# Windowed attention and a soft mixture of experts: re-ordered steps, sums from a column of ones, masks written by TensorE, and a second layer by column halves

## The chip, the cores and the metric

One core of a Trainium2 chip. The metric is device time of one execution in microseconds, from start to end of the program; the times of the kernel before are three runs, and one execution was recorded by the hardware profiler. All data begin and end in device memory. The core's engines are TensorE (PE; PEld is its weight load), VectorE (DVE), ScalarE (ACT), GpSimd (POOL) and SyncE (SP), which here issues all transfers. Every engine works through its own list of instructions in order.

## The reference

```
q, k, v: (4, 8, 768, 64);  n_sink = 4, window = 128
scores = q @ k.T / 8;  keep key p for query s if p < 4 or 0 <= s - p < 128
a = softmax(scores);   att = a @ v                     # (4, 8, 768, 64)
x = att.transpose(0, 2, 1, 3).reshape(3072, 512)
logits = x @ phi                                       # (3072, 32): 8 experts x 4 slots
d = softmax(logits over the 3072 tokens);  slot_input = d.T @ x        # (32, 512)
h = relu(slot_input[e] @ w1[e]);  slot_out[e] = h @ w2[e]              # F = 1024
out = softmax(logits over the 32 slots) @ slot_out                     # (3072, 512) f32
```

Inputs and outputs are f32. The expert weights are 2 x 16 MB of f32, the output is 6 MB.

## The kernel before, in words

**Attention** runs in 12 jobs (batch b of 4, and j of 3 blocks of 256 queries; `window_path`, from L694). A job loads k, q and v in blocks of 128 rows (`load`, 256 KB each), transposes k and q on PE into `kt` and `qt` (`prep`), and makes four score tiles (`softmax`: `quad` is the group of heads, `odd` the half of a block's queries). For each tile PE makes the scores, DVE masks them in PSUM and takes the row maxima (`maxima`), ACT takes four exponentials with their row sums (`exps`: an ACTIVATE and a read of the accumulator each), DVE adds the sinks' share and inverts the sums (`inverse`), POOL multiplies the tile by the inverses (128x528, key `N`) and copies out the sink columns (`sinks`). In jobs with j = 0 there are no earlier keys, and DVE fills those columns with a large negative number by MEMSET. Then PE transposes the weights (`weights_transposed`), POOL cuts them to the window (`select`: 8 AFFINE_SELECT in a job, 7 where j = 0), PE multiplies them by v (`values`), and the result x is turned back (`natural`).

**Router** (`Moe.tokens`, L348), still inside the job: logits, running maxima over tokens, the exponentials with their sum (`zb`), the products d.T @ x added up in `acc` (`sums`), and the running sum `z` (`totals`). `finish` (L439) makes the slots' inputs; `slot_softmax`, `stack` and `turn` make the weights with which the output is combined.

**Order.** Nothing of this is issued as written. Each step is entered in `Plan` with a key, engines on which it may run ("AV" means ACT or DVE), a time, and what it reads and writes; `Plan.order` (L175) plays the steps through, takes at each point the free engine that can start first and the ready step of the lowest key, and so sets each engine's list and the engine of a step that has a choice. The keys are the hand-made numbers of `CFG`. The helper at L129 issues every planned instruction, so that nearly all of the profile has that one line.

**Weights** come as 32 tiles of 1 MB in the order of `Weights` (L639), into SBUF tiles of 1 MB (`slot`, 22 of them, and the two tiles `first` in which k, q, x and x's transpose lie during attention). 18 are issued before attention ends, the rest as its tiles become free.

**Tail** (`tail`, L552), in the written order: layer 1 (64 matmuls of 512 columns, tiles 0 to 15), relu, transposes of h into `ht`, layer 2 (`second`: one step is four matmuls of 512 columns side by side in four column groups; expert groups r = 0, 1, and k = 0 to 7 in each; the last four k by column halves, from tiles 28 to 31, each of which holds all columns of two experts for two k). Its result, 32 slots x 512, is split into a rounded part and a remainder for both halves (L620 on ACT, L621 on DVE), and 24 products of 48 matmuls make the output: one for each 128 tokens, copied from PSUM by ACT and DVE in turn (L635), and stored by 2 transfers of 512 KB and 5 of 1 MB (L636).

## Time and profile before

| | us |
|---|---|
| median of 3 runs (lowest, highest) | 240.36 (239.79, 242.28) |
| profiled execution, its own time | 240.57 |
| its span in the trace | 238.9 |
| PE busy, share of the span | 203.1, 85% |
| DVE, ACT, POOL busy | 157.3, 147.7, 140.4 |
| transfers, mean over the span | 249 GB/s |

The trace covers 238.9 of the 240.57 us; 1.67 us lie outside it. Rows below give starts in us from the start of the span. A group such as `ps<-wt` names what an instruction writes and reads: `ps` is PSUM, `wt` any tile from `slot`, `first` the two tiles of k, q and x. A releaser after `<-` is what ended the idle time before an instruction. Idle time of an engine that is not the bottleneck costs nothing. Matmuls run at two records for each f32 instruction, so that counts of PE in the trace are about twice those of the program.

### The profile page before, as it was taken

The page shows a single profiled execution, that of the slowest core. Times are in us where ns is not written, and L with a number is a line of the kernel's source. Part 1 is how long each engine was busy: PE and PEld are TensorE (multiplying, and loading weights), DVE is VectorE, ACT ScalarE, POOL GpSimd, SP SyncE. Part 2 cuts the span into 40 slices and gives each one's busy share as a digit, 9 for nine tenths or more (in the row PEclk, how much of TensorE's full clock was granted, in tenths as well). Part 3 has the DMA queues.
Part 4 walks back from the last instruction along what each step waited for, and adds up shares of the span by engine and source line. Part 5 has one row for each costly group of instructions (what it writes and reads, how often), then busy time and mean ns, then how long its engine had stood idle before and what let it go on. Part 6 is the DMA issues. An engine that isn't in the chain of part 4 may idle for free.

```text
span 238.9 us, 9509 instructions
## 1 busy us (share of the span) xinstructions
PE 203.1 (85%) x3754; PEld 143.5 (60%) x3754; DVE 157.3 (66%) x444; ACT 147.7 (62%) x584; POOL 140.4 (59%) x281
## 2 busy tenths in 40 slices
PE   7864999998999889999999999989699999987600
PEld 7844676876768575768677676857375325236600
DVE  4198878779898967999987999896327105005800
ACT  2187487977889878788987778996325103005600
POOL 2018799793998887698978698989933320000000
PEclk9997699999999999999999999999899999998965
DMA  5596968789998899598999999793549999922994
GB/s 118 118 178 137 255 189 196 291 192 292 276 209 241 217 345 203 190 227 243 208 348 214 296 265 201 255 408 114 176 144 420 375 420 416 411 110 86 399 394 187
DMA packets 84502, 59.49 MB, mean 249 GB/s; under 512 B 76260, under 2 KB 76260, under 8 KB 82916
## 3 DMA queue, kind: packets, MB, share of 16 engines
q1 hardware_dynamic: 84452, 58.83, 81.8%
q8 instruction: 31, 0.51, 0.9%
q14 instruction: 19, 0.16, 0.2%
HBM read 52.53 MB, written 6.29 MB: 246 GB/s over the span
## 4 chain that ended last, share of the span: by engine, by line
PE 52%; DVE 18%; DMA 8%; ACT 7%; issue 7%; POOL 2%; SPq 0%; DVEq 0%; ACTq 0%; POOLq 0%
PE ps L129 51%; DMA wt<-in_moe_w_dram 8%; DVE wt L129 6%; DVE ps L129 5%; ACT wt L129 4%; POOL wt L129 2%; PE ps L1254 2%; DVE rs L129 1%; DVE wt L635 1%; DVE first L129 1%; DVE sums L129 1%; DVE acc L129 1%; ACT pt L129 1%; ACT qt L129 1%; DVE qt L129 0%
## 5 line engine op out<-in xcount | busy, mean ns | idle before, releaser
L129 PE MATMUL ps<-wt 64*64 64x192 f32 (+6 forms) x1214 | 58.2, 314 | 2.8 <-DVE wt L621 1.5
L129 POOL TENSOR_TENSOR wt<-wt 128x528 f32<-128x528 f32 (+1 forms) x72 | 47.1, 663 | 21.1 <-DVE wt L129 15.1
L129 POOL TENSOR_SCALAR_AFFINE_SELECT wt<-wt 128x512 f32<-128x512 f32 x88 | 53.6, 637 | 5.3 <-ACT wt L129 4.8
L129 ACT ACTIVATE wt<-ps,wt 128x132 f32<-128x132 f32 x144 | 51.3, 375 | 8.7 <-DVE wt L129 7.1
L129 PEld LDWEIGHTS ps<-wt 64*64 64x64 f32 (+3 forms) x1214 | 40.8, 137 | 17.0 <-issue 6.9
L129 PE MATMUL ps<-wt,qt 64*64 64x196 f32 (+2 forms) x780 | 46.7, 333 | 3.3 <-ACT qt L129 2.1
L129 PEld LDWEIGHTS ps<-wt,qt 64*64 64x64 f32 x780 | 30.1, 138 | 14.6 <-ACT wt L129 4.9
L129 DVE TENSOR_REDUCE wt<-ps 128x4 f32<-128x528 f32 x48 | 34.0, 707 | 1.7
L129 ACT COPY wt<-ps 128x512 f32<-128x512 f32 x42 | 24.2, 594 | 16.2 <-PE ps L129 12.7
L129 ACT ACTIVATION_READ_ACCUMULATOR wt<-ps,wt 128x1 f32 x144 | 30.2, 210 | 0.0
L129 PE MATMUL ps<-ident,wt 64*128 64x64 f32 (+1 forms) x370 | 25.7, 241 | 3.5 <-DVE wt L129 3.1
L129 PE MATMUL ps<-ident,first 64*128 64x64 f32 (+1 forms) x560 | 25.5, 230 | 3.0 <-ACT wt L129 1.1
L129 PEld LDWEIGHTS ps<-ident,wt 64*128 64x128 f32 (+1 forms) x370 | 20.3, 146 | 11.4 <-POOL wt L129 6.8
L129 PEld LDWEIGHTS ps<-ident,first 64*128 64x128 f32 (+1 forms) x560 | 21.9, 141 | 6.4 <-ACT wt L129 2.3
L129 DVE COPY first<-ps 128x512 f32<-128x512 f32 x23 | 15.6, 686 | 12.3 <-PE ps L129 11.9
L129 DVE COPY_PREDICATED ps<-later,ps 128x256 f32<-128x256 uint8 x48 | 20.3, 423 | 2.7 <-PE ps L129 1.5
L129 DVE COPY wt<-ps 128x512 f32<-128x512 f32 x30 | 20.2, 683 | 1.9 <-PE ps L129 1.1
L129 ACT COPY first<-ps 128x512 f32<-128x512 f32 x25 | 14.9, 601 | 9.4 <-issue 6.9
L129 ACT ACTIVATE pt<-ps,wt 128x132 f32<-128x132 f32 x48 | 17.3, 386 | 1.5 <-DVE wt L129 1.2
L129 POOL TENSOR_TENSOR pt<-pt,wt 128x528 f32<-128x528 f32 x12 | 13.1, 1090 | 1.6 <-ACT wt L129 0.8
L129 PE MATMUL ps<-wt,si 128*32 128x512 f32 x120 | 13.9, 593 | 0.0
L129 PE MATMUL ps<-first,phi 128*32 128x128 f32 x384 | 13.4, 276 | 0.3
(119 smaller groups left out, 255.3 us busy)
## 6 DMA issues: line engine op xcount, KB each, us to landing
wt<-in_moe_w_dram SPq DMA_DIRECT2D x30, 1024.0 KB, 8.4
wt<-in_v_dram SPq DMA_DIRECT2D x24, 256.0 KB, 5.3
first<-in_k_dram SPq DMA_DIRECT2D x22, 256.0 KB, 4.4
first<-in_q_dram SPq DMA_DIRECT2D x22, 256.0 KB, 4.8
out_dram<-wt SPq DMA_DIRECT2D x5, 1024.0 KB
first<-in_moe_w_dram SPq DMA_DIRECT2D x2, 1024.0 KB
out_dram<-wt SPq DMA_DIRECT2D x2, 512.0 KB, 2.7
first<-in_k_dram SPq DMA_DIRECT2D x4, 128.0 KB, 2.4
```

The costliest lines, as they stand in the source:

```text
L129: return self.tc.keep_in_program_order(f(*args, **kw))
L635: (nc.vector.tensor_copy if i else nc.scalar.copy)(ob[:, n - n0, i], yp)
L1254: nc.tensor.matmul(t[:, 0:P], lhsT=c.ident, rhs=c.ident, start=True, stop=True)
```

## The change

It has seven parts.

1. The keys of `CFG` are other numbers, so that every engine's list is in another order, and steps with a choice may run on another engine.
2. In jobs with j = 0 PE writes the large negative number: after each score matmul of such a block another one, of two constant bf16 tiles (`never`), adds -2^15 x 2^9 x 64 to the masked columns. DVE's MEMSET is gone, and the two predicated copies for the sinks become one by a mask `seen`.
3. The tokens' matrix x has a column of ones behind each half, so that the products (257 columns) give the sums also. `totals`, `zb` and the read of the accumulator in `tokens` are gone.
4. The sums of two tiles are inverted together (24 pairs of 128x8 in place of 48 of 128x4). The multiplication may run on POOL (one instruction) or ACT (four of 128x132), as the plan picks. It picks ACT in 12 of 48, the fourth of each job; and ACT for 3 of the 8 copies of the last block of `kt`. Of the copies with a choice between ACT and DVE more go to DVE (of `qt` 11 of 24, before 5).
5. In `values` the second pass multiplies the sinks last (one change of PE's tile shape less).
6. The tail: layer 2 runs all by column halves. The last four tiles hold, two by two, columns 0:256 and 256:512 of experts 4 to 7, each loaded by two transfers of 512 KB whose runs in memory are 1 KB long. The split and the combination of the first six blocks' left columns stand ahead of the last two tiles' work; the first 8 of 12 blocks of 256 tokens are stored by halves (16 transfers of 256 KB, runs of 1 KB), the last four by 512 KB (runs of 4 KB). The transposes of h stand inside layers 1 and 2.
7. `pts` and the small sums have tiles of their own, there are 21 slots, and the tiles of `kt` and `v` are given to weights where before those of `pts` were. 18 tiles are still issued before attention ends, and 14 after.

```diff
...
+    c.never = pool.tile([P, 192], BF16, name="never")
+    nc.vector.memset(c.never[:, 0:64], -2.0 ** 15)
+    nc.vector.memset(c.never[:, 64:192], 2.0 ** 9)
...
-        plan.add(next(k), "A", 0.46,
-                 lambda e: nc.scalar.activation(lt[64:128], L["tile"][64:128, 0:P], AF.Exp, bias=new[64:128],
-                                                accum_out=zb[64:128]),
-                 r=[L["name"], ("m", n % 2)], w=["lt1", zbn], last=L)
+        plan.add(next(k), "A", 0.4,
+                 lambda e: nc.scalar.activation(lt[64:128], L["tile"][64:128, 0:P], AF.Exp, bias=new[64:128]),
+                 r=[L["name"], ("m", n % 2)], w=["lt1"], last=L)
...
-                nc.tensor.matmul(S["tile"][32 * g:32 * g + 32, 0:256], lhsT=lhs, rhs=rhs, start=True, stop=True)
...
+                nc.tensor.matmul(S["tile"][32 * g:32 * g + 32, 0:257], lhsT=lhs, rhs=rhs, start=True, stop=True)
...
-                nc.vector.scalar_tensor_tensor(acc, acc, al, S["tile"][:, 0:256], op0=ALU.mult, op1=ALU.add)
+                nc.vector.scalar_tensor_tensor(acc, acc, al, S["tile"][:, 0:257], op0=ALU.mult, op1=ALU.add)
...
-        def totals(e):
...
-                nc.vector.tensor_scalar(z[64:128], z[64:128], al[64:128], zb[64:128], op0=ALU.mult, op1=ALU.add)
...
-        plan.add(next(k), "V", 0.3, totals, r=[zbn, aln], w=["z"])
...
+            if k == 1:
+                turned(0)
...
-        def second(r, k, c0=0, c1=512):
...
+        def second(r, k, h):
             for j in range(4):
-                if t < 28:
-                    w, o = wts[t + j], 512 * (k % 4)
+                if r == 0 or k < 4:
+                    w, o = wts[16 + 8 * r + 4 * (k // 4) + j], 512 * (k % 4) + 256 * h
                 else:
-                    w, o = wts[28 + 2 * (k % 4 // 2) + j // 2], 1024 * (j % 2) + 512 * (k % 2)
-                nc.tensor.matmul(op[32 * j:32 * j + 32, c0:c1], lhsT=ht[:, k, r, j].rearrange("p q i -> p (q i)"),
-                                 rhs=w[:, o + c0:o + c1], start=(r == 0 and k == 0), stop=(r == 1 and k == 7),
+                    w, o = wts[28 + 2 * h + k % 4 // 2], 1024 * (k % 2) + 256 * j
+                nc.tensor.matmul(op[32 * j:32 * j + 32, h, 0:256], lhsT=ht[:, k, r, j].rearrange("p q i -> p (q i)"),
+                                 rhs=w[:, o:o + 256], start=(r == 0 and k == 0), stop=(r == 1 and k == 7),
                                  skip_group_check=True)
 
-        for r in range(2):
-            for k in range(8 - 4 * r):
-                second(r, k)
-
-        for h in range(2):
-            for k in range(4, 8):
-                second(1, k, 256 * h, 256 * h + 256)
-        for h in range(2):
-            o = slice(256 * h, 256 * h + 256)
-            hi, x = tw[:, 0, o], op[:, o]
+        def split(h):
+            hi, x = tw[:, 0, 256 * h:256 * h + 256], op[:, h, 0:256]
             nc.scalar.copy(hi, x)
-            nc.vector.scalar_tensor_tensor(tw[:, 1, o], hi.bitcast(F32), c.lo_rows, x, op0=ALU.mult, op1=ALU.add)
-
+            nc.vector.scalar_tensor_tensor(tw[:, 1, 256 * h:256 * h + 256], hi.bitcast(F32), c.lo_rows, x,
+                                           op0=ALU.mult, op1=ALU.add)
...
-        for n0, n1 in ((0, 1), (1, 2), (2, 4), (4, 6), (6, 8), (8, 10), (10, 12)):
-            ob = slot()[:, 0:1024 * (n1 - n0)].rearrange("p (n i m) -> p n i m", n=n1 - n0, i=2)
-            for n in range(n0, n1):
-                for i in range(2):
...
-                    (nc.vector.tensor_copy if i else nc.scalar.copy)(ob[:, n - n0, i], yp)
-            nc.sync.dma_start(ov[:, n0:n1], ob)
...
+        def combine(n, h):
+            if h == 0 and n % 2 == 0:
+                obs.append(slot().rearrange("p (n i m) -> p n i m", n=2, i=2))
+            cols, yp, ob = slice(256 * h, 256 * h + 256), pool.tile(), obs[n // 2][:, n % 2]
+            for i in range(2):
+                nc.tensor.matmul(yp[:, 256 * i:256 * i + 256], lhsT=self.ct[n // 3][:, n % 3, i, :], rhs=tw[:, 1, cols],
+                                 start=(i == 0), stop=(i == 1), skip_group_check=True)
+            (nc.vector.tensor_copy if (n + h) % 2 else nc.scalar.copy)(
+                ob[:, :, cols], yp.rearrange("p (i m) -> p i m", i=2))
+            if n < HALF:
+                nc.sync.dma_start(ov[:, n, :, cols], ob[:, :, cols])
+            elif h:
+                nc.sync.dma_start(ov[:, n], ob)
+
+        for k in range(8):
+            second(0, k, 0)
+            if k == 1:
+                turned(1)
+        for k in range(4):
+            second(1, k, 0)
+        for k in range(8):
+            second(0, k, 1)
+        for k in range(4, 8):
+            second(1, k, 0)
+        split(0)
+        for k in range(4):
+            second(1, k, 1)
+        for n in range(HALF - 2):
+            combine(n, 0)
+        for k in range(4, 8):
+            second(1, k, 1)
+        split(1)
+        for n in range(HALF - 2, HALF):
+            combine(n, 0)
+        for n in range(HALF):
+            combine(n, 1)
+        for n in range(HALF, 12):
+            combine(n, 0)
+            combine(n, 1)
...
-        self.order += [(2, 4 + 2 * j, h) for h in (2, 3) for j in range(2)]
+        self.order += [(2, k, h) for h in range(2) for k in (4, 6)]
...
-            t2 = t.rearrange("p (e m) -> p e m", e=2)
-            w = self.w2[e:e + 2].rearrange("e (p k) m -> p e (k m)", p=P)[:, :, 1024 * h:1024 * h + 1024]
+            w = self.w2[4:8].rearrange("e (p k) m -> p e k m", p=P)[:, :, e:e + 2, 256 * h:256 * h + 256]
+            for k in range(2):
+                self.nc.sync.dma_start(t[:, 1024 * k:1024 * k + 1024].rearrange("p (e m) -> p e m", e=4), w[:, :, k])
+            self.tiles.append(t)
+            return
         self.nc.sync.dma_start(t2, w)
...
+HALF = 8
...
-CFG = {'prep': [19.45, -187.13, -2.19, 131.09, -1.42, 7.11],
...
+CFG = {'prep': [32.39, 3.55, -7.31, 216.98, 231.66, -112.18],
...
-    slots = ctx.enter_context(tc.tile_pool(name="slots", bufs=NSLOT - 2))
+    slots = ctx.enter_context(tc.tile_pool(name="slots", bufs=NSLOT - 3))
...
-            add(key[0], "G", 0.55, lambda e: nc.gpsimd.tensor_copy(ktb[:, :, 0, 4:132], ktb[:, :, 2, 4:132]),
+            add(key[0], "GA", (0.55, 0.51), lambda e: (nc.scalar.copy if e == "A" else nc.gpsimd.tensor_copy)(
+                ktb[:, :, 0, 4:132], ktb[:, :, 2, 4:132]),
...
+                        if lo:
+                            nc.tensor.matmul(s["tile"][0:64, u, 196 * x:196 * x + lo], lhsT=c.never[p, 0:64],
+                                             rhs=c.never[p, 64:64 + lo], start=False, stop=(x == 1), skip_group_check=True)
...
-            if j == 0:
-
-                r0, r1 = slice(0, 64), slice(64, P)
-                nc.vector.memset(sv[r0, :, :, 0:68] if odd else sv[r0, :, :, 0:128], NEG)
-                if not odd:
-                    for r, x in ((r0, 0), (r1, 1)):
-                        nc.vector.copy_predicated(sv[r, :, :, 128:132], where(x, r, 4),
-                                                  c.neg[r].unsqueeze(1).unsqueeze(1).to_broadcast([64, 2, 2, 4]))
-            nc.vector.copy_predicated(own if odd else old, where(odd), old if odd else own)
+            where = c.later[:, odd].unsqueeze(1).unsqueeze(1).to_broadcast([P, 2, 2, 64])
+            if j == 0 and not odd:
+                nc.vector.copy_predicated(sv[:, :, :, 128:132], c.seen.unsqueeze(1).unsqueeze(1).to_broadcast([P, 2, 2, 4]),
+                                          c.neg.unsqueeze(1).unsqueeze(1).to_broadcast([P, 2, 2, 4]))
+            nc.vector.copy_predicated(own if odd else old, where, old if odd else own)
...
-        add(keys["N"], "V", 0.33, inverse, r=[zn], w=[zn])
-        add(keys["N"], "G", 1.08, lambda e: nc.gpsimd.tensor_tensor(
-            pt, pt, z.unsqueeze(2).to_broadcast([P, 4, 132]), op=ALU.mult), r=[zn, pn], w=[pn])
...
+        add(keys["N"], "V", 0.36, inverse, r=[("ze", 2 * quad), ("ze", 2 * quad + 1)], w=[zn])
+        def normal(e, x):
+            t = pair[:, :, 132 * x:132 * x + 132]
+            if e == "A":
+                for a in range(4):
+                    nc.scalar.mul(t[:, a], t[:, a], z[:, 4 * x + a:4 * x + a + 1])
+            else:
+                nc.gpsimd.tensor_tensor(t, t, z[:, 4 * x:4 * x + 4].unsqueeze(2).to_broadcast([P, 4, 132]), op=ALU.mult)
+
+        for x in range(2):
+            add(keys["N"], "GA", (1.04, 1.1), lambda e, x=x: normal(e, x), r=[zn, ("pt", 2 * quad + x)], w=[("pt", 2 * quad + x)])
...
-                part(first)
+                for f in (sunk, part) if first else (part, sunk):
+                    f(first)
...
-    add(100.0, "D", 0.0, lambda e: moe.place(slot(), [0, 1], 2),
...
+    add(100.0, "D", 3.0, lambda e: weight(),
+        w=["kt0", ("kts", 0), ("kts", 1), "v4s"] + [("kt", i, y) for i in range(2) for y in range(2)])
...
-    add(100.0, "D", 3.0, lambda e: weight(), w=[("pt", x) for x in range(PT)] + [("z", x) for x in range(4)] + ["vsink", "v4s"])
+    add(100.0, "D", 0.0, lambda e: moe.place(fr.tile([P, 2112], F32, name="pts")[:, 0:2048], [0, 1], 2), w=[("place", 0)] + [("pt", x) for x in range(4)])
...
+    add(100.0, "D", 3.0, lambda e: weight(), w=[("vb", x) for x in range(4)])
```

**DVE in the first job.** The list of DVE from its first score tile to the first sum of row sums, before (`ps` are the scores, `wt` the small sums):

```order
L129 MEMSET ps 64x2x2x128
L129 COPY_PREDICATED ps<-later,neg 64x2x2x4 x2
L129 COPY_PREDICATED ps<-later,ps 128x2x2x64
L129 TENSOR_REDUCE wt<-ps 128x2x2
L129 MEMSET ps 64x2x2x68
L129 COPY_PREDICATED ps<-later,ps 128x2x2x64
L129 TENSOR_REDUCE wt<-ps 128x2x2
L129 MEMSET ps 64x2x2x128
L129 COPY_PREDICATED ps<-later,neg 64x2x2x4 x2
L129 COPY_PREDICATED ps<-later,ps 128x2x2x64
L129 TENSOR_REDUCE wt<-ps 128x2x2
L129 TENSOR_REDUCE wt<-wt 128x4
```

and in the change (`small` are the small sums):

```order
L136 COPY_PREDICATED ps<-seen,neg 128x2x2x4
L136 COPY_PREDICATED ps<-later,ps 128x2x2x64
L136 TENSOR_REDUCE small<-ps 128x2x2
L136 COPY_PREDICATED ps<-later,ps 128x2x2x64
L136 TENSOR_REDUCE small<-ps 128x2x2
L136 COPY phi<-acc 128x32 x4
L136 COPY_PREDICATED ps<-seen,neg 128x2x2x4
L136 COPY_PREDICATED ps<-later,ps 128x2x2x64
L136 TENSOR_REDUCE small<-ps 128x2x2
L136 COPY_PREDICATED ps<-later,ps 128x2x2x64
L136 TENSOR_REDUCE small<-ps 128x2x2
L136 TENSOR_REDUCE small<-small 128x8
```

The MEMSETs (a fourth follows below the rows) and the 64-row copies are gone from ahead of the maxima, two copies for all rows are new, and the sum for two tiles at once (`128x8`, its reciprocal follows) stands behind all four maxima; before, the sum for one tile stood behind three. Four copies of `phi`, which stood behind the first job's maxima, are now inside the stretch.

**POOL in the last job.** From its third multiplication on, before (the multiplications are `128x528`, the `CAST` and the small `TENSOR_TENSOR` are sinks):

```order
L129 TENSOR_TENSOR wt<-wt 128x528
L129 CAST wt<-wt 128x2x16
L129 TENSOR_TENSOR wt<-wt 128x2x16
L129 CAST wt<-wt 128x2x16
L129 TENSOR_TENSOR wt<-wt 128x2x16
L129 TENSOR_TENSOR pt<-pt,wt 128x528
L129 AFFINE_SELECT wt<-wt 128x4x128
L129 CAST wt<-pt 128x2x16
L129 TENSOR_TENSOR wt<-pt,wt 128x2x16
L129 AFFINE_SELECT wt<-wt 128x4x128 x7
```

and in the change (`pts` are the weights before they are turned):

```order
L136 TENSOR_TENSOR pts<-pts,small 128x4x132
L136 CAST small<-pts 128x2x16
L136 TENSOR_TENSOR small<-pts,small 128x2x16
L136 CAST small<-pts 128x2x16
L136 TENSOR_TENSOR small<-pts,small 128x2x16
L136 AFFINE_SELECT wt<-wt 128x4x128 x8
```

The fourth multiplication is no longer on POOL; it is an `ACTIVATE pts<-pts,small 128x132 x4` of ACT's list. The eight selections stand in one row behind all sinks.

**PE and SP in the tail.** PE from layer 2's last shared part to the end, before (`32x...` is layer 2, `128x256` the combination):

```order
L129 MATMUL ps<-wt 32x512 x17
L129 MATMUL ps<-wt 32x256 x32
L129 MATMUL ps<-wt 128x256 x24
L129 MATMUL ps<-wt,qt 128x256 x12
L129 MATMUL ps<-wt 128x256 x12
```

and in the change:

```order
L136 MATMUL ps<-wt 32x256 x33
L136 MATMUL ps<-wt,pts 128x256 x12
L136 MATMUL ps<-wt 32x256 x16
L136 MATMUL ps<-wt,qt 128x256 x4
L136 MATMUL ps<-wt,pts 128x256 x12
L136 MATMUL ps<-wt,qt 128x256 x8
L136 MATMUL ps<-wt 128x256 x12
```

Twelve combining matmuls, those of the first six blocks' left columns, stand ahead of the last 16 of layer 2; before, all 48 stood behind it. SP's last transfers, before:

```order
L129 DMA wt<-in_moe_w_dram 128x2048 x4
L129 DMA first_75<-in_moe_w_dram 128x2048
L129 DMA wt<-in_moe_w_dram 128x2048 x5
L129 DMA wt<-in_moe_w_dram 128x2x1024 x4
L636 DMA out_dram<-wt 128x1024 x2
L636 DMA out_dram<-wt 128x2x1024 x5
```

and in the change:

```order
L136 DMA wt<-in_moe_w_dram 128x2048 x4
L136 DMA first_75<-in_moe_w_dram 128x2048
L136 DMA wt<-in_moe_w_dram 128x2048 x5
L136 DMA wt<-in_moe_w_dram 128x4x256 x8
L638 DMA out_dram<-wt 256x1x256 x16
L640 DMA out_dram<-wt 128x1024 x4
```

The loads up to the last four tiles keep their number and shape; these become 8 transfers, and the stores 20.

## Rows read from the trace of the kernel before

**Rows 1.** Stages: length; busy (count) PE, PEld, DVE, ACT, POOL; PEclk, DMA, GB/s

```profile
0.00:31.20 31.20, 22.88 (x263) 18.57 (x265) 19.91 (x72) 16.00 (x64) 13.10 (x34) 0.89 0.76 169
31.20:160.00 128.80, 120.93 (x2755) 90.41 (x2751) 111.70 (x306) 109.62 (x455) 106.54 (x203) 1.00 0.91 248
160.00:176.50 16.50, 13.69 (x302) 10.46 (x299) 7.31 (x22) 7.11 (x29) 12.59 (x26) 0.90 0.42 139
176.50:210.70 34.20, 33.95 (x345) 14.85 (x346) 9.78 (x33) 7.77 (x27) 8.16 (x19) 1.00 0.99 396
210.70:219.60 8.90, 6.37 (x76) 4.16 (x69) 2.48 (x5) 2.34 (x5) 0.00 (x0) 0.95 0.04 14
219.60:236.50 16.90, 5.30 (x34) 5.05 (x33) 6.12 (x10) 4.81 (x9) 0.00 (x0) 0.70 0.96 375
```

**Rows 2.** DVE by time, first job: start, duration, shape, count, idle before

```profile
15.03 0.48 DVE L129 MEMSET ps<- 64x512 f32 x1
...
19.26 0.68 DVE L129 COPY wt<-ps 128x512 f32<-128x512 f32 x1
...
23.43 1.31 DVE L129 COPY phi<-acc 128x32 f32<-128x32 f32 x4
```

**Rows 3.** PE by time, first job, same columns

```profile
13.33 1.56 PE L129 MATMUL ps<-wt,qt 64*64 64x68 f32 x32 [0.83 <-ACT qt L129]
...
20.08 0.24 PE L129 MATMUL ps<-ident,wt 64*128 64x64 f32 x1 [3.11 <-DVE wt L129]
```

**Rows 4.** Groups by shape: count, busy us, mean ns of one, idle before

```profile
L129 DVE MEMSET ps<- 64x512 f32 x8 | 3.9, 485 | 8.2 <-PE ps L129 6.7 <-ACT sums L129 1.1
L129 DVE MEMSET ps<- 64x272 f32 x8 | 2.3, 285 | 0.4
L129 DVE COPY_PREDICATED_SCALAR ps<-later,neg 64x16 f32 x16 | 3.8, 237 | 0.6
L129 DVE COPY_PREDICATED ps<-later,ps 128x256 f32<-128x256 uint8 x48 | 20.3, 423 | 2.7 <-PE ps L129 1.5 <-ACT sums L129 0.4
L129 DVE TENSOR_REDUCE wt<-ps 128x4 f32<-128x528 f32 x48 | 34.0, 707 | 1.7
L129 DVE TENSOR_REDUCE wt<-wt 128x4 f32<-128x8 f32 x48 | 7.3, 153 | 2.2 <-ACT pt L129 1.1 <-ACT wt L129 0.7
L129 DVE RECIPROCAL wt<-wt 128x4 f32<-128x4 f32 x48 | 8.6, 178 | 1.7
L129 POOL TENSOR_TENSOR wt<-wt 128x528 f32<-128x528 f32 x36 | 38.1, 1066 | 18.2 <-DVE wt L129 15.1 <-PE ps L129 1.4 <-ACT wt L129 1.4
L129 ACT ACTIVATE wt<-ps,wt 128x132 f32<-128x132 f32 x144 | 51.3, 375 | 8.7 <-DVE wt L129 7.1 <-POOL wt L129 1.0
```

**Rows 5.** POOL by time, last job

```profile
164.65 1.07 POOL L129 TENSOR_TENSOR pt<-pt,wt 128x528 f32<-128x528 f32 x1
...
168.14 2.98 POOL L129 TENSOR_SCALAR_AFFINE_SELECT wt<-wt 128x512 f32<-128x512 f32 x5 [0.16 <-ACT wt L129]
```

**Rows 6.** PE by time, tail

```profile
199.94 0.64 PE L129 MATMUL ps<-wt 128*32 128x512 f32 x4
...
212.73 2.78 PE L129 MATMUL ps<-wt 128*32 128x256 f32 x44 [1.00 <-DMA wt<-in_moe_w_dram]
```

**Rows 7.** Chain of waits, tail: start, duration, engine, tile, line

```profile
215.56 0.38 ACT wt L620
215.96 0.49 DVE wt L621
...
217.42 5.01 PE ps L129 x27
```

**Rows 8.** Loads of q, k, v, then of weights; columns of rows 1

```profile
92.00:93.00 1.00, 0.97 (x15) 0.50 (x13) 0.97 (x2) 0.89 (x5) 0.96 (x2) 1.00 1.03 229
...
202.00:204.00 2.00, 2.00 (x24) 0.65 (x20) 0.00 (x0) 0.00 (x0) 0.00 (x0) 1.00 1.03 416
```

More of the change, by code (lines that the diff above doesn't have):

```diff
@@ L372, in logits @@
                                      skip_group_check=True)
-        plan.add(next(k), "P", 0.87, logits, r=xs + ["phi"], w=[L["name"]], new=L, mode=(128, 32), size=64)
+        plan.add(next(k), "P", 0.9, logits, r=xs + ["phi"], w=[L["name"]], new=L, mode=(128, 32), size=64)
         key = next(k)
@@ L1089, in more @@
             weight()
-    more(NSLOT - 2 - len(wts))
-    weights.load(moe.first[1])
+    weights.load(moe.first[1][:, 0:2048])
     moe.nc = Core(tc, ("tensor",))
@@ L1213, in general_path @@
     for i in range(2):
-        weights.load(moe.first[i])
+        weights.load(moe.first[i][:, 0:2048])
     def more(n):
```

235 lines of the change are left out of this document (115 added, 120 removed).

## The prediction

> **What bounds the kernel now.** I read the stages first [rows 1]. From 31.2 to 160.0 us ten jobs pass, 12.88 us each; PE is busy for 120.93 of 128.80 us, so that all its idle time there is 7.87 us, 6.1%. DVE, ACT and POOL stand at 83 to 87%: attention is PE's, and the other three are close enough behind it to make it wait for short times only. From 176.5 to 210.7 transfers and PE are both full (share 0.99, PE 33.95 of 34.20): 13 weight tiles, 2.63 us each. From 210.7 to 219.6 hardly a byte moves (share 0.04, 8.90 us), and from 219.6 the stores run at 0.96 up to 236.5. So the tail is a stream of transfers with one hole of 8.90 us. What fills the hole is seen in PE's list [rows 6] and the chain [rows 7]: the last tile lands at 212.73, 2.03 us after the bytes end; PE needs 2.78 us for the six half steps of layer 2 left, the split of both halves takes from 215.56 to 217.42, and the first store's bytes come 2.18 us after the first combining matmul (219.60 - 217.42). At the start, PE waits 3.11 us up to 20.08 for one copy of DVE [rows 3], which DVE does at 19.26, behind the masks and maxima of four tiles [rows 2]. In the last job POOL's work runs unbroken but for 0.16 us to its last selection, which ends at about 171.1 [rows 5].
>
> All sums are against the profiled execution's 240.57 us (span 238.9 and 1.67 outside), which is 0.21 above the median of the three runs.
>
> **Masks and start, -1.4 us.** In the first job DVE needs from 15.03 to 19.26, 4.23 us, for the third tile, the first two inverses and the fourth tile ahead of the copy that PE waits for [rows 2]. By the new list there are two tiles, one copy for the sinks and one paired inverse: 0.24 + 2 x (0.42 + 0.71) + 0.33 = 2.83 us [rows 4], 1.4 less. The four copies of phi, 1.31 us [rows 2], move into this list between the second and the third tile. Two tiles now take 0.24 + 2 x 1.13 = 2.5 us in place of about 3.9, and the third tile's scores are not there before 14.89 (13.33 + 1.56) [rows 3]: the copies fall into that gap. Without this cover they cost 1.3, and the term is nothing. The 64 new matmuls of `never` stand on PE: two tiles' scores, 32 records, take 1.56 us [rows 3], so one record is 0.05 us, and 64 of one record each at most 3.1 us over four jobs, at least nothing where they run beside the others. I put 0.8 of it into the next term.
>
> **Steady attention, -3 us.** DVE loses 3.9 + 2.3 of MEMSET, half of 3.8 for the sinks, and half of 7.3 + 8.6 for the inverses [rows 4], 16 us in twelve jobs, plus the running sums; copies that it takes from ACT give back about half. POOL loses 12 multiplications of 1.066 us [rows 4], 12.8 us. ACT gets these as 48 instructions of 128x132, 0.375 us each where they read PSUM [rows 4], 18 us by that row as the upper bound, 12.8 if they were as quick as on POOL. With the copies given to DVE ACT stays below 12 us in a job of 12.88. So the engine that PE waits for least often may become ACT, and the two others have room. What this is worth at the end is only PE's idle time: at best all 7.9 us. At worst PE gets the 3 us of the new matmuls and nothing in return, +3. I take 0.3 us a job, somewhat over a third of the idle time, net of the matmuls: the waits in it are many and short, and a list in another order removes some and makes others. The moved mode switch in `values` is inside this.
>
> **Last job, -0.8 us.** POOL's unbroken chain loses one multiplication of 1.07 us [rows 5]; ACT does it in about 1.5, beside POOL's other three. All of it if nothing else ends later, nothing if ACT's four end last.
>
> **Tail, -2.7 us.** The steps, on the times of before.
> - Loads. A packet of q, k, v is 256 bytes: at 229 GB/s over 16 engines one takes 17.9 ns; a packet of weights is 4 KB: at 416 GB/s 157.5 ns [rows 8]. On the straight line between them 1 KB takes 45.8 ns, against 39.4 for a quarter of 4 KB: 6.4 ns more. Four tiles are 4.19 MB, 256 packets of 1 KB per engine, +1.65 us; the loads end at 210.7 + 1.65 = 212.35.
> - PE. From 199.94 to 211.73, where it waits for the last tiles, PE did 26 half steps [rows 6], 0.45 us each; a full step costs as much as two halves, so halving is free. It now has 20 half steps before it needs tiles 28 and 29: 199.94 + 9.1 = 209.0 (the transposes moved into layers 1 and 2 are the same number). Tile 29's bytes end at 212.35 - 2 x 3.04 = 206.3 (2.63 + 0.41 for each of two tiles), landed at 208.3: no wait. The left half is done at 210.8, its split (0.38 + 0.49 and hand-overs, 0.9) at 211.7, four half steps of the right half at 212.6. Then the first combining matmul runs, which before ran at 217.42. With the same 2.18 us the first bytes go out at 214.8.
> - The hole is 214.8 - 212.35 = 2.45 in place of 8.90: -6.45. Six left columns are 1.57 MB, 4.4 us at the 1 KB rate (16 x 1024 bytes in 45.8 ns, 358 GB/s), until 219.2. The right half: tile 31 lands at 212.35 + 2.03 = 214.4, 1.8 us of half steps once the twelve matmuls ahead have their PSUM tiles (about 214.8), split 0.9, 2.18 to the next bytes: 219.7. A second hole of 0.5.
> - Stores. 16 of 256 KB are 4.19 MB, again +1.65; the other four keep 4 KB.
> - -6.45 + 3.3 + 0.5 = -2.65, rounded -2.7. For the 1 KB packets the lower bound is no cost (the rate of 4 KB), the upper one the cost per byte of 256-byte packets, 71.6 ns, 32.2 more x 512 = 16.5 us. I take the line, as it passes through both.
>
> The Trainium skill (DMA: Bandwidth & Descriptors, section "Why small descriptors are slow (HBM only)") gives a fixed overhead of about 3 cycles for each packet of 32-byte beats; by that rule 1 KB needs 35 cycles against 32.75 for a quarter of 4 KB, an estimated 1.4 us for all in place of 3.3, and the sum would be 1.9 lower. The trace speaks for the dearer line: by the rule a 256-byte packet would take an estimated 13.2 ns where rows 8 give 17.9.
>
> **Sum:** -1.4 - 3.0 - 0.8 - 2.7 = -7.9, and 240.57 - 7.9 = **232.7 us**.
>
> **Rivals.**
> - *Attention gives nothing*: PE's waits only change their causes. Then start, last job and tail stay, -4.9: 235.7, and 237.9 with the tail alone. For it: PE has 6.1% to give, and three engines are all near it. Against it: DVE and POOL together lose some 29 us of work, and nobody else gains as much. 0.20.
> - *Attention gives all*: 232.7 + 3 - 7.9 = 227.8. 0.13.
> - *The tail's hole stays*: if the split of the left half waits behind ACT's or DVE's other work, or the twelve early matmuls hold PE's in-order list until PSUM tiles come free, the hole shrinks by less than the packets cost. If it doesn't shrink at all, 240.57 - 5.2 + 3.3 = 238.7. The six copies of 0.6 to 0.7 us on two engines speak against it: they are done by 214.8. 0.06.
> - *ACT becomes the bound (slower)*: the 48 multiplications stand in ACT's in-order list ahead of exponentials and copies that PE needs. Each set of four holds that list for 1.5 us. If all of it lands on PE, 18 us, and the gains of attention and last job go too: 240.57 - 4.1 + 18 = 254.5. It decides from the point where 6.3 of the 18 us land on PE's path, over a third (242.8). For it: ACT is at 85% and its exponentials release DVE and POOL; against it: the plan gives ACT only the fourth tile of a job, and moves copies off it. 0.05, at about 245.
> - *1 KB packets cost as 256-byte ones per byte (slower)*: +13.2 on the forecast, 245.9. From 45.8 + 7.9 / 0.512 = 61 ns for a packet on, the change gains nothing. 0.04.
> - *A fixed price for each transfer (slower)*: there are 17 more (4 loads, 13 stores). If each held up the queue for the 2.03 us that pass between the last byte and its reader [rows 1, 6], that were 34 us and 266 in all. Rows 8 speak against it: transfers of 256 KB follow each other at a share of 1.03. 0.02. The Trainium skill (DMA: Bandwidth & Descriptors, section "Bandwidth") has this as a rule, to batch to 1 MiB or more for 75% of peak, with about 2 us fixed for one transfer.
>
> **Numbers.** The forecast, 230 to 235, has 0.50. The range of 8 in 10 goes from 227.5 to 237.5: the forecast, nearly all of "attention gives nothing" and most of "gives all". A measurement of this kernel tells about 1%: 238.0 and 242.8. Faster than that: the forecast, both cases of attention, 0.83, and a little of the tail's case, 0.84; within 1%: 0.09; slower: 0.07, half of it ACT's.
>
> **What would show it.** Right: less than 3 us without transfers between the last load and the first store, loads of 2.63 us up to tile 27 and about 3.0 for the last four, stores of 1 KB at some 360 GB/s; a period of 12.6 us or less between jobs; the first job's wait of PE shorter by 1 to 1.5 us. Wrong: PE waiting for ACT after the fourth tile of each job, ACT over 12.3 us in a job; a hole of 5 us or more; 1 KB packets at 60 ns or more; a PE that does layer 1 late, so that tile 28 waits for it and not it for tile 28.

## The result, and the profile after

The changed kernel takes 233.11 us (median of 4 runs, 232.71 to 235.15) against 241.32 us of the kernel before beside it (239.79 to 243.53): a ratio of 0.970 [0.960, 0.979]. Measured again later (a_again) it took 234.03 us (232.96 to 235.80) against 240.51, 0.974 [0.968, 0.980]. Some executions run in a slower state, and all ratios leave these out, so that a ratio is not always that of the medians. The forecast was 232.7, the range 227.5 to 237.5. The profiled execution took 233.21 us, 7.4 less than that of before, with a span of 231.4.

The stages, cut at the same events as in [rows 1] (first `values`, `values` of the eleventh job, transfers and PE both full, end of the loads, first store); columns as there:

```profile
0.00:25.60 25.60, 19.52 (x266) 16.44 (x266) 15.12 (x61) 14.54 (x56) 10.77 (x32) 0.93 0.74 166
25.60:155.40 129.80, 119.23 (x2801) 92.33 (x2801) 104.26 (x253) 114.11 (x477) 95.41 (x191) 1.00 0.88 249
155.40:172.00 16.60, 14.04 (x325) 10.61 (x329) 10.48 (x26) 9.54 (x39) 12.67 (x28) 1.00 0.55 189
172.00:207.20 35.20, 34.76 (x449) 17.68 (x440) 9.44 (x32) 7.10 (x23) 7.17 (x17) 1.00 1.01 380
207.20:209.60 2.40, 2.40 (x32) 2.00 (x32) 1.62 (x3) 1.56 (x3) 0.00 (x0) 1.00 0.03 11
209.60:229.00 19.40, 6.09 (x60) 4.90 (x48) 6.21 (x11) 5.09 (x10) 0.00 (x0) 0.79 0.95 328
```

Two things stand out. The hole without transfers is 2.40 us where it was 8.90, and the stores behind it take 19.40 where they took 16.90. And the ten steady jobs became no shorter: 129.80 us for 128.80. DVE, ACT and POOL together do 313.8 us there in place of 327.9, but PE's idle time rose from 7.87 to 10.57 us. What attention gained lies at its beginning: `values` of the first job starts at 25.6 and not 31.2 (at 27.0 in the trace of a_again).

DVE in the first job (timeline: start, duration, shapes, count), which answers to [rows 2]:

```profile
13.73 0.24 DVE L136 COPY_PREDICATED_SCALAR ps<-seen,neg 128x16 f32 x1 [0.48 <-PE ps L136]
...
15.54 0.71 DVE L136 TENSOR_REDUCE small<-ps 128x4 f32<-128x528 f32 x1
...
16.36 0.20 DVE L136 RECIPROCAL small<-small 128x8 f32<-128x8 f32 x1
17.33 0.69 DVE L136 COPY wt<-ps 128x512 f32<-128x512 f32 x1 [0.77 <-PE ps L136]
```

From the third tile to the copy that PE waits for it is now 3.60 us (13.73 to 17.33), 0.77 of it idle; before 4.23. The work in it is 2.83 us. PE (same columns), to be held against the 3.11 us of [rows 3]:

```profile
16.48 0.71 PE L136 MATMUL ps<-ident,first 64*128 64x64 f32 x15 [1.43 <-ACT pts L136]
18.16 0.28 PE L136 MATMUL ps<-ident,pts 64*128 64x64 f32 x2 [0.97 <-DVE wt L136]
18.86 0.72 PE L136 MATMUL ps<-ident,pts 64*128 64x64 f32 x14 [0.42 <-POOL pts L136]
```

The one long wait became three short ones of 2.82 us together. The chain of waits in the tail (start, duration, engine, tile, line), which answers to [rows 7]:

```profile
177.85 32.91 PE ps L136 x418
...
210.78 0.38 ACT wt L621
...
211.19 0.49 DVE wt L622
...
211.72 3.84 PE ps L136 x28
```

Before, the last tiles' landing stood in the way; now PE works from the first matmul of layer 1 (177.85, before 183.43) to the split of the right half without a pause, and the chain runs over PE.

### The profile page after: what moved, and what is told of

Its sections match the earlier page's. It is cut to its first block, busy times and chain, and to the rows that moved or that the text cites. A ratio compares the mean times of both kernels' runs of the same rounds, so it can differ in the third digit from the quotient of the medians.

```text
span 231.4 us, 9764 instructions
## 1 busy us (share of the span) xinstructions
PE 196.0 (85%) x3912; PEld 144.0 (62%) x3912; DVE 147.1 (64%) x383; ACT 151.9 (66%) x605; POOL 126.0 (54%) x266
## 4 chain that ended last, share of the span: by engine, by line
PE 51%; ACT 17%; DVE 12%; issue 7%; POOL 6%; DVEq 0%; ACTq 0%; POOLq 0%
PE ps L136 50%; ACT pts L136 8%; ACT wt L136 3%; DVE ps L136 3%; DVE small L136 2%; POOL pts L136 2%; ACT first L136 2%; DVE wt L136 2%; POOL wt L136 2%; PE ps L1291 2%; ACT lt L136 1%; DVE vsink L136 1%; DVE qt L136 1%; ACT qt L136 1%; DVE first L136 1%
## 5 line engine op out<-in xcount | busy, mean ns | idle before, releaser
L136 ACT ACTIVATE pts<-ps,small 128x132 f32<-128x132 f32 x192 | 68.1, 392 | 6.1 <-DVE small L136 3.4
L136 POOL TENSOR_SCALAR_AFFINE_SELECT wt<-wt 128x512 f32<-128x512 f32 x88 | 52.8, 634 | 3.0 <-ACT wt L136 1.2
L136 POOL TENSOR_TENSOR pts<-pts,small 128x528 f32<-128x528 f32 x36 | 38.2, 1076 | 29.3 <-DVE small L136 20.9
L136 PE MATMUL ps<-wt 64*64 64x192 f32 (+4 forms) x1278 | 52.5, 298 | 1.6 <-issue 0.3
L136 PEld LDWEIGHTS ps<-wt 64*64 64x64 f32 (+2 forms) x1278 | 38.9, 129 | 12.5 <-issue 4.8
L136 ACT ACTIVATION_READ_ACCUMULATOR pts<-ps,small 128x1 f32 x192 | 43.9, 229 | 0.0
L136 DVE TENSOR_REDUCE small<-ps 128x4 f32<-128x528 f32 x48 | 33.9, 707 | 1.6
L136 DVE COPY wt<-ps 128x512 f32<-128x512 f32 x33 | 22.3, 682 | 4.8 <-ACT wt L136 2.1
L136 PE MATMUL ps<-ident,pts 64*128 64x64 f32 (+1 forms) x396 | 20.2, 233 | 3.7 <-DVE wt L136 2.1
L136 PEld LDWEIGHTS ps<-ident,pts 64*128 64x128 f32 (+1 forms) x396 | 16.3, 142 | 9.7 <-POOL small L136 5.6
L136 ACT ACTIVATE pts<-pts,small 128x132 f32<-128x132 f32 x48 | 15.9, 437 | 0.6 <-DVE small L136 0.6
L136 POOL TENSOR_TENSOR small<-pts,small 128x32 f32<-128x32 f32 x48 | 12.1, 252 | 3.9
```

What stands on the lines that cost most here:

```text
L136: return self.tc.keep_in_program_order(f(*args, **kw))
```

## The experiments

Medians (lowest, highest; runs), the ratio to the kernel before on the same chip with its 95% interval, and two times in the profiled execution: start of layer 1, and span.

| kernel | median us | ratio | layer 1 | span |
|---|---|---|---|---|
| before (first profile) | 240.36 | 1 | 183.4 | 238.9 |
| changed | 233.11 (232.71, 235.15; 4) | 0.970 [0.960, 0.979] | 177.9 | 231.4 |
| a_again, the same program | 234.03 (232.96, 235.80; 6) | 0.974 [0.968, 0.980] | 180.7 | 233.5 |
| e1 changed, old tail | 235.29 (234.72, 236.55; 6) | 0.979 [0.975, 0.984] | 178.5 | 233.4 |
| e2 before, new tail | 237.47 (236.36, 241.19; 6) | 0.986 [0.980, 0.992] | 182.5 | 235.2 |
| f_before, fillers | 238.20 (236.99, 241.09; 12) | 0.992 [0.988, 0.996] | 179.2 | 235.8 |
| f_after, fillers | 234.03 (233.72, 237.55; 6) | 0.974 [0.969, 0.980] | 179.1 | 232.6 |
| e4 changed, POOL multiplies | 235.79 (235.30, 236.44; 6) | 0.976 [0.971, 0.981] | 180.2 | 233.6 |
| e5 changed, MEMSETs again | 240.69 (239.01, 242.87; 12) | 0.996 [0.993, 1.000] | 188.0 | 241.1 |
| m1 before, new masks | 235.68 (233.38, 238.57; 6) | 0.976 [0.969, 0.982] | 179.0 | 234.3 |
| m3 before, new masks and tail | 234.90 (233.26, 236.32; 6) | 0.978 [0.972, 0.984] | 178.1 | 231.9 |
| m2 as m3, fillers, two queues | 236.71 (234.31, 238.98; 6) | 0.977 [0.970, 0.985] | 180.9 | 233.5 |
| x1 changed, two queues | 234.01 (232.00, 235.37; 6) | 0.966 [0.960, 0.972] | 180.9 | 233.6 |
| x2 as x1, combining earlier | 232.11 (231.62, 234.79; 6) | 0.968 [0.962, 0.974] | 177.8 | 230.2 |

The row a_again says how a single trace may be read: the same program reached layer 1 2.8 us later than in its first profile. An interval is about 1.5 us to either side. The traces of e5 and x1 are of the longest of their executions (242.87 and 235.37 us).

### Attention or tail: e1_old_tail, e2_tail_alone

e1 is the changed kernel with `tail` and the last tiles of `Weights` as they were:

```
-        self.order += [(2, k, h) for h in range(2) for k in (4, 6)]
+        self.order += [(2, 4 + 2 * j, h) for h in (2, 3) for j in range(2)]
```

> The changed attention with the tail of before (its layer 2, its last four weight tiles, its stores). Theory of the prediction: the new tail is worth 2.7 us and works by itself, so this takes 233.1 + 2.7 = 235.8, and the stretch without transfers before the first store is about 8.9 us again. Rival: the shorter hole comes from attention's earlier end, not from the tail's order; then 233.1 and a hole near 2.5. Second rival: 1 KB packets cost more than the early stores give; then under 233.

e2 is the other half: the kernel before with the new `tail` and these tiles.

> The attention of before with the new tail alone. Theory: -2.7 us against before (about 238.6 where before takes 241.3), a hole of 2.5 us in place of 8.9. Rival (the tail needs the earlier end of attention): no change.

By the ratios attention alone gives 5.0 us (e1) and the tail alone 3.4 (e2); what e1 lacks to the changed kernel is 2.3 by the first result and 1.3 by a_again. The forecast had 5.2 and 2.7. The hole in e1's windows (columns as in rows 1):

```profile
207.00:209.00 2.00, 2.00 (x40) 1.23 (x42) 0.00 (x0) 0.00 (x0) 0.00 (x0) 1.00 0.04 8
209.00:211.00 2.00, 1.01 (x13) 0.39 (x5) 0.48 (x1) 0.62 (x2) 0.00 (x0) 1.00 0.00 0
211.00:213.00 2.00, 1.47 (x12) 1.31 (x12) 1.12 (x3) 1.01 (x3) 0.00 (x0) 0.98 0.00 0
213.00:215.00 2.00, 2.00 (x12) 2.00 (x11) 1.93 (x4) 1.56 (x4) 0.00 (x0) 0.50 0.53 211
```

Six us with hardly a byte, and more at both ends. In e2 what was moved in each of 40 slices of 0.78 us, from 205 us on:

```profile
GB/s 348 363 340 349 350 346 353 299 129 59 21 0 329 344 340 348 342 340 348 344 338 330 356 296 272 207 365 346 398 354 411 418 418 407 396 122 58 0 0 0
```

Three slices are nearly empty, some 2.4 us. So the hole goes with the tail's form and with nothing in attention.

### PE's clock after a wait: f_before_fillers, f_after_fillers

In the trace of before PE's granted clock falls to its low level, 1.2 GHz (0.50 of 2.4), right behind the wait of 3.11 us. Fillers are useless matmuls of 128x128 in that wait; the lists stay as they are.

```
+            if n == 0 and quad == 0:
+                plan.marks[len(plan.steps)] = (18, filler)
...
+    def filler(bank):
+        nc.tensor.matmul(bank[:, 0:P], lhsT=c.ident, rhs=c.ident, start=True, stop=True)
```

> The kernel before, every engine's list as it was, with 18 matmuls of no use (128x128, into a free PSUM bank) on PE ahead of the step for which it waits 3.11 us in the first job; they fill some 2.5 us of that wait. Theory that PE's clock is the missing part of the start: the trace of before shows PEclk 0.50 from about 20.7 to 27.5 right behind this wait, with PE busy for most of it; with the wait filled the clock stays at 1.00 and the kernel gains 1.5 to 3.4 us (237.9 to 239.8 where before takes 241.3). Rival (the first job is bound by DVE, ACT and POOL, PE's speed there costs nothing): no gain, 0 to +0.5 us, even if the clock stays up.

The windows of the kernel before (PEclk is the third column from the right):

```profile
18.00:20.00 2.00, 0.00 (x0) 0.00 (x0) 1.93 (x5) 0.82 (x6) 1.94 (x3) 1.00 0.97 216
20.00:22.00 2.00, 1.56 (x25) 1.45 (x27) 1.01 (x7) 1.95 (x10) 1.68 (x4) 0.68 0.86 172
22.00:24.00 2.00, 1.32 (x21) 1.02 (x21) 1.97 (x5) 1.61 (x4) 1.40 (x2) 0.50 0.12 28
24.00:26.00 2.00, 2.00 (x28) 1.24 (x20) 1.66 (x6) 0.00 (x0) 1.84 (x6) 0.50 1.04 235
```

and with the fillers:

```profile
18.00:20.00 2.00, 2.00 (x20) 2.00 (x19) 1.93 (x7) 0.77 (x4) 1.92 (x5) 1.00 0.91 206
20.00:22.00 2.00, 2.00 (x41) 1.86 (x40) 0.81 (x4) 2.00 (x10) 1.31 (x3) 1.00 0.85 182
22.00:24.00 2.00, 1.26 (x32) 1.06 (x32) 1.97 (x5) 1.30 (x3) 1.69 (x2) 1.00 0.35 78
24.00:26.00 2.00, 1.89 (x44) 1.15 (x36) 1.93 (x8) 0.87 (x3) 1.77 (x7) 1.00 1.23 255
```

PE idle at 18 to 20 us is followed by half the clock, PE kept at work is not, and `values` of the first job starts at 29.1 in place of 31.3. The ratio gives 1.9 us, with an interval of 0.9 to 2.8. So in the kernel before a wait of PE at the start costs more than its length: a cost that the prediction did not have.

f_after is the changed kernel with 7 fillers in its wait for DVE's copy (0.97 us above).

> The changed kernel with its lists as they are and 7 matmuls of no use on PE in its wait of 0.97 us in the first job. Clock theory: the stretch at PEclk 0.50 (about 19.6 to 22.4) goes, worth 0.5 to 1.4 us (231.7 to 232.6). Rival: the clock falls anyway, since the wait of 1.43 us ahead of it is not filled; then 233.1 to 233.4.

Its clock stays at 1.00 from 16 to 28 us, where the changed kernel's trace has 0.50 from 20 to 22, and it is no faster: 0.974 against 0.970 and 0.974. After the change the clock at the start is worth nothing that these runs can tell from zero.

### Multiplications on POOL, MEMSETs on DVE: e4_mult_pool, e5_memset

e4 is the changed kernel, its order kept, with all 48 multiplications on POOL.

```
-            fn(e)
+            fn("G" if i in self.to_pool else e)
```

> The changed kernel with all 48 multiplications on POOL, the 12 of ACT put into POOL's list at their planned places; nothing else moves. Theory (POOL's relief carries part of attention's gain): slower, +1 to +3 us, the last job's 1.07 in it. Rival 1 (ACT, at 88% in the steady stretch, is what PE waits for): faster, -1 to -2 us. Rival 2 (neither engine sets the end of a job): 233.1, no difference but the last job's, under 1 us.

0.976 against 0.970 and 0.974: by the ratios 0.6 to 1.6 us slower, with intervals that overlap. From 25 to 155 us ACT is busy for 103.97 us and POOL for 104.80 (changed kernel, nearly the same stretch: 114.11 and 95.41), and the last job's fourth tile has its maxima at 158.2 us, between the 157.1 and 158.5 of the changed kernel's two traces. That leaves up to some 1.5 us open, says that the whole term of 3 us does not come from here, and shows nothing of rival 1.

e5 is the changed kernel with DVE's MEMSETs in place of PE's `never` matmuls; the single copy for the sinks and the order stay.

```
+            if j == 0:
+                nc.vector.memset(sv[0:64, :, :, 0:68] if odd else sv[0:64, :, :, 0:128], NEG)
...
-                            nc.tensor.matmul(s["tile"][0:64, u, 196 * x:196 * x + lo], lhsT=c.never[p, 0:64],
```

> The changed kernel with DVE's MEMSETs ahead of the maxima again in place of PE's extra matmuls (16 MEMSETs; the single copy for the sinks stays); all lists otherwise as they are. Theory: in the first job the four MEMSETs lie on the path, 2 x 0.49 + 2 x 0.29 = 1.5 us, and the longer wait of PE keeps its clock down longer: +1.5 to +3 us (234.6 to 236). Rival: the gap before the third tile's scores takes two of them, and later jobs level the rest: under +0.5 us.

It takes nearly the time of the kernel before: 0.996, 6.4 us more than the changed kernel by the ratios (5.4 against a_again's). None of the expectations reached that far. The groups by shape (count; busy us, mean ns) of e5:

```profile
L136 DVE MEMSET ps<- 64x512 f32 x8 | 3.9, 485 | 5.6 <-PE ps L136 4.9
L136 DVE MEMSET ps<- 64x272 f32 x8 | 2.3, 285 | 1.5 <-PE ps L136 1.2
```

6.2 us of MEMSET cost 5.4 to 6.4 us at the end. The table by job in the next part shows where.

### The masks alone, and the parts together: m1_masks_alone, a_again, m2_all_but_order, m3_masks_tail

m1 is the kernel before, its own lists, with PE's `never` matmuls and the single copy for the sinks (8 copies of 128 rows for 16 of 64) and nothing else:

```
+                        if lo:
+                            nc.tensor.matmul(s["tile"][0:64, u, 196 * x:196 * x + lo], lhsT=c.never[p],
+                                             rhs=large[p, 0:lo], start=False, stop=(x == 1), skip_group_check=True)
...
-                nc.vector.memset(sv[r0, :, :, 0:68] if odd else sv[r0, :, :, 0:128], NEG)
```

> The kernel before with the masks alone changed: PE's extra matmuls and the single copy for the sinks in place of DVE's 16 MEMSETs and 16 64-row copies, every list in the old order. In the changed kernel the MEMSETs cost 6.6 us when put back, as much as their own 6.2 us on DVE. Theory M (in a job with j = 0 DVE's list sets the end, whatever the order): -5 to -7 us, about 235. Rival (the old order was made around the MEMSETs, and only the first job has them on its path): -1.4 to -2.5, about 239.

> The changed kernel once more, beside the others of this set: 0.97 of before, 233 us.

The masks alone bring 0.976, 5.9 us, as theory M had it: all that attention gains in the changed kernel (5.0 by e1). m3 adds the new tail to m1.

> The kernel before, its own lists, with two parts of the change: the masks written by PE (as in m1) and the new tail (as in e2), without the fillers and the second store queue of m2. Theory that the two gains lie on different parts of the path and add: -5.9 (m1) and -3.4 (e2) give 9.3, a ratio of about 0.962, or 0.968 if both runs flattered their parts by the spread seen between runs of one program (1.5 us in all); then the new order, the multiplications on ACT, the paired inverses and the sums by a ones column bring the changed kernel nothing. Theory that an earlier end of attention isn't worth its full length to the tail: not below m1 by more than 1 us, 0.972 to 0.976, as m2 was; in the trace the first combining matmul would then not be earlier than in e2 by the 3.5 us by which layer 1 starts earlier, with PE waiting for the last tiles or the last loads ending late.

0.978 [0.972, 0.984]: by the ratios not faster than m1, and not to be told from the changed kernel. The theory that the gains add, 0.962 to 0.968, is missed. The sign of the other theory isn't there either: in m3's trace the first combining matmul comes as long after the start of layer 1 as in e2's (29.4 us), and so 4.4 us earlier. The last job's maxima of the fourth tile, in the timelines of DVE: before,

```profile
161.09 0.71 DVE L129 TENSOR_REDUCE wt<-ps 128x4 f32<-128x528 f32 x1
```

changed,

```profile
157.06 0.71 DVE L136 TENSOR_REDUCE small<-ps 128x4 f32<-128x528 f32 x1
```

m1,

```profile
158.04 0.71 DVE L135 TENSOR_REDUCE wt<-ps 128x4 f32<-128x528 f32 x1
```

m3,

```profile
155.82 0.71 DVE L135 TENSOR_REDUCE wt<-ps 128x4 f32<-128x528 f32 x1
```

m1 and m3 have the same attention and differ by 2.2 us here. 1.94 of it is one pause of PE in m1, for which the profile shows no cause (timeline of PE):

```profile
60.15 0.78 PE L135 MATMUL ps<-ident,first 64*128 64x64 f32 x19 [1.94 <-issue]
```

In the same place of m3 PE works through. With that known, masks alone bring attention at least as far as the whole change did. In sum the new order, the paired inverses, ACT's multiplications and the column of ones bring nothing that these runs can tell from zero. The new code with the old keys (e3), which was to separate the order, gave no result, so that of these parts only ACT's has a run of its own (e4).

By job the sum has two sides. The time gained in each job, from the starts of the maxima of its fourth tile (minus is time lost; jobs 0, 3, 6 and 9 have j = 0):

| job | 0 | 1 | 2 | 3 | 4 | 5 | 6 | 7 | 8 | 9 | 10 | 11 | all |
|---|---|---|---|---|---|---|---|---|---|---|---|---|---|
| m3 against before | 2.9 | -0.1 | 0.0 | 2.4 | -0.8 | 0.0 | 2.3 | -1.2 | -0.2 | 1.1 | -1.0 | -0.1 | 5.3 |
| changed against before | 3.1 | 0.9 | 0.6 | 2.8 | -1.3 | -1.6 | 2.9 | -1.9 | 0.4 | 0.8 | -1.4 | -1.3 | 4.0 |
| changed against e5 | 1.7 | 0.3 | 0.4 | 2.2 | 0.0 | 0.0 | 2.3 | -1.2 | 0.0 | 1.7 | 0.0 | 0.0 | 7.4 |

Each row gains in the four jobs with j = 0 (against a_again's trace e5 loses 6.0 in all, not 7.4). In m3, by the masks, 8.7 us are gained there and 3.0 given back in the jobs right behind. The changed kernel has the same steps, and it loses 1.6 us in job 5 and 1.3 in job 11, where m3 loses next to nothing. All eight traces with the new lists have these two losses (1.6 to 1.8 and 1.3 to 1.5), and the three with the old lists and the new masks don't (0.2 at most). So the rest of the change is not idle: it costs time in some jobs of the steady stage, and which part does it was not tried.

In the traces m3's span is 7.0 us below that of before: 5.3 up to the last job's fourth tile and 1.6 from layer 1 on, where e2 alone has 2.8. In the ratios 5.9 and 3.4 come to 5.4 together. Each has about 1.5 us of interval, which explains a part; the rest stays open.

m2 adds the fillers and a second queue for stores to m3:

> The old order with the masks, the new tail with its stores on two queues in turn, and the 18 matmuls in PE's first wait. If the gains add up (masks by theory M 6, tail 3.4, queues 0.5 to 1, the matmuls up to 1.9 less what the masks already take of that wait): 230 to 232, less than the changed kernel, and then its new order, the paired inverses, ACT's multiplications and the column of ones bring nothing. Rival (masks worth 2 in the old order): 234 to 235.5.

The 230 to 232 us were missed. By the ratio, 0.977, m2 is level with m3, 0.978: neither the fillers nor the second queue add anything that can be told, though m2's clock stays at 1.00 at the start where m3's falls to 0.50 from 20 to 24 us.

### The stores: x1_two_queues, x2_early

In the changed kernel SP issues a store in some 0.57 us, but the 5th, 12th and 17th took 1.5 to 1.7, and the stream of stores thins out at these places. x1 issues from SP and ACT in turn:

```
+            q = nc.sync if (n + h) % 2 else nc.scalar
...
-                nc.sync.dma_start(ov[:, n, :, cols], ob[:, :, cols])
+                q.dma_start(ov[:, n, :, cols], ob[:, :, cols])
```

> The changed kernel with the 20 stores issued by two queues in turn: those whose last copy ACT makes by ACT, the others by SP. In the changed kernel SP takes 0.57 us for most stores but 1.5 to 1.7 us for the 5th, 12th and 17th, and each time transfers fall to less than half for about 1 us some 1.4 us later. Theory (the holes come from SP's slow issues): with two queues the holes go, -1.0 to -1.5 us (231.6 to 232.1). Rival 1 (the queue is only full, the holes are of the transfers themselves): no difference. Rival 2 (issuing delays ACT's copies): slower, up to +1.5.

The GB/s in 40 slices, of the changed kernel from 205 to 232 us,

```profile
GB/s 335 317 194 62 5 0 24 337 364 322 335 155 237 346 349 335 341 357 323 328 138 231 354 319 360 334 329 272 402 411 401 401 401 419 401 115 18 12 0 0
```

and of x1 from 205 to 234:

```profile
GB/s 347 349 349 363 333 281 172 75 21 0 120 326 363 318 336 347 331 349 333 346 332 348 343 339 346 348 343 397 397 396 384 396 390 396 316 136 40 0 0 0
```

The dents at 155, 138 and 272 GB/s are gone, so the smaller holes were the issuing queue's and not a late right half's. In time it gives nothing that can be told: from the start of layer 1 to the end x1 takes 52.7 us, the changed kernel 53.6 and 52.8 in its two traces, and the interval of the ratio, 0.966, overlaps both of its intervals.

x2 is x1 with all eight left columns combined after two half steps of the right half instead of six after four:

```
-        for k in range(4):
+        for k in range(2):
             second(1, k, 1)
-        for n in range(HALF - 2):
+        for n in range(HALF):
             combine(n, 0)
-        for k in range(4, 8):
+        for k in range(2, 8):
             second(1, k, 1)
...
```

> The changed kernel with stores on two queues and the left columns of all first eight blocks combined two half steps after the split, not four: the first store 0.9 us sooner, and 8 in place of 6 halves to send until the right half is ready. Theory: the early hole falls from 2.4 to 1.5 us, no new hole, 231.5 to 232.3. Rival (PE's list waits for PSUM tiles behind eight copies, and the right half comes later by what the left gains): as with two queues alone, 232 to 234.

It has the lowest median of all, 232.11, within the theory's range, and takes 52.4 us from layer 1 to the end. Its first store is issued 29.9 us after the start of layer 1, in the changed kernel 30.5, and its stretch below 100 GB/s is 2.0 us long (207.0 to 209.0) where the changed kernel's is 2.5: an early hole that is shorter, by half of what was expected. It ran on the same chip as a_again (234.03); the intervals of the two ratios overlap, so that a gain is not shown.

## Why the prediction was right, step by step

The total was right within 0.4 us and the tail by its steps. Attention's sum, -5.2, was right (5.0 by e1) while its three terms were not.

- **Tail, -2.7: right in mechanism, and in size as far as it can be told.** It measures 1.3 to 2.3 taken away (e1) and 3.4 alone (e2). With attention's forecast of -5.2 taken off its times, the loads were to end at 207.15 and the first combining matmul to run at 207.4, with a hole of 2.45 us; the trace has about 207.2, 207.21 and 2.40. A 1-KB packet was to take 45.8 ns. The first combining matmuls in PE's timeline, and a window in the last four tiles' loads:

```profile
207.21 1.65 PE L136 MATMUL ps<-wt,pts 128*128 128x256 f32 x12
...
200.00:205.00 5.00, 5.00 (x100) 3.03 (x96) 0.00 (x0) 0.00 (x0) 0.00 (x0) 1.00 1.10 350
```

  16 x 1024 bytes at 350 GB/s are 46.8 ns. The straight line between the two rows was a good guide. The rival of the 256-byte price falls by the same row. That of a fixed price for each transfer falls by the stores: outside the three dents, 16 transfers of 256 KB follow each other at 319 to 364 GB/s.

  By the Trainium skill (DMA: Bandwidth & Descriptors, section "Why small descriptors are slow (HBM only)"), with its 3 cycles for each packet, 1 KB would cost an estimated 7% more per byte than 4 KB. The trace does not agree: with 350 GB/s against 416 it costs 19% more.
- **The second hole, +0.5: the cause was another.** There was no late right half, but three slow issues of SP, as x1 shows.
- **Masks and start, -1.4: the step that failed, in size.** It priced DVE's MEMSETs only where PE's long wait showed them, in the first job, and put the rest of their 6.2 us among work that hides. They are on the path in all four jobs with j = 0, as the table by job shows: m1 gives 5.9 us for the masks alone, e5 takes back 5.4 to 6.4 for the MEMSETs. The account that fits is that in such a job no tile has its maxima until DVE has filled it, ACT's exponentials wait for the maxima and PE's transposes for ACT. PE's idle time does not show the price: m3's ten steady jobs are 2.5 us shorter than before (126.31 for 128.80), and PE's idle time in them falls by 1.0 (7.87 to 6.86).

  In the first job DVE's work came out as forecast, 2.83 us, but PE's wait did not become 1 to 1.5 us shorter: 2.82 us in three pieces for 3.11 in one. The first job's fourth tile is 3.1 us earlier all the same. The clock is no part of this in m3, whose fourth tile is 2.9 earlier: its rows at 18 to 26 us have 0.63, 0.50, 0.50 and 0.66, and those of before at 20 to 28 us 0.68, 0.50, 0.50 and 0.62.
- **Steady attention, -3.0: wrong.** The time per job is 12.98 us and not 12.6 or less. Between the first job's and the last job's fourth tile the changed kernel gains 0.9 us; from the first job's `values` to the eleventh's it loses 1.0. (The two differ as the lists are in another order.) By the table it gains 6.5 us in jobs 3, 6 and 9, which are the masks', and loses 5.6 in the others. ACT's load was inside its bounds: a multiplication took 437 ns from start to end, but they overlap, and 48 keep ACT busy for 15.9 us, where the forecast had 12.8 to 18 (groups by shape):

```profile
L136 ACT ACTIVATE pts<-pts,small 128x132 f32<-128x132 f32 x48 | 15.9, 437 | 0.6 <-DVE small L136 0.6
```

  With 114.11 us in ten jobs, 11.4 in a job of 12.98, ACT stays under the 12.3 that was to show it as the bound. The rival in which it becomes one falls, and e4 without these multiplications is no faster. The rival "attention gives nothing" was right about this term and would have been wrong on the sum, as the masks paid for it.
- **Last job, -0.8: nearly all of it is the clock's chance.** Layer 1 starts 5.6 us earlier where the last job's fourth tile is 4.0 earlier, so 1.6 are gained between the two. But PE's clock falls there in some traces and not in others, of one program too. Before, changed and a_again:

```profile
172.00:174.00 2.00, 2.00 (x44) 1.45 (x36) 0.00 (x0) 0.00 (x0) 1.28 (x4) 0.50 0.04 12
...
168.00:170.00 2.00, 1.89 (x70) 1.62 (x64) 0.00 (x0) 0.00 (x0) 1.56 (x5) 1.00 0.00 0
...
168.00:170.00 2.00, 1.88 (x30) 1.51 (x34) 0.07 (x1) 0.00 (x0) 1.83 (x6) 0.52 0.00 0
```

  With the clock at 1.00 all the way, layer 1 starts 21.0 us after that tile's maxima in all four such traces with the old lists and 20.8 to 21.3 after in four with the new ones. Where the clock falls it is 22.3 in the two with the old lists (before, m3) and 22.0 to 22.2 in three with the new (a_again, e4, x1), 23.5 in e5. At the same clock the new lists gain some 0.2 us, and e4, which gives the multiplication back to POOL, is no later than the others (22.0).

That -1.4 was too small and -3.0 and -0.8 too large, and that they make up for each other, is luck.

## What to carry to other kernels

Price work that is taken off an in-order engine in every place where the next engine waits for its result, not only where a long wait is printed: here 6.2 us of MEMSETs were priced at 1.4 and worth 5.4 to 6.4. Judge a lighter load by the length of the stage that it is in: here three engines lost 14 us and the ten jobs became 1 us longer. Compare the clock of two traces before a difference of 1 to 2 us between them is explained. Split a last layer by output columns, so that stores begin before the last weights are used, and price the shorter runs by the rows of the packet sizes on either side.
